# An attention stage ordered by a planner: its delays and occupancies replaced, and 14 transposes of the identity put first

## The chip, the cores and the metric

The kernel runs on one core of a Trainium2 chip. Its time is the device time in microseconds (us) of one execution. Five engines work in parallel, each through its own queue in a fixed order: TensorE (PE, with its weight loads shown as PEld), VectorE (DVE), ScalarE (ACT), GpSimd (POOL), and SyncE (SP), which issues the DMAs. An instruction that has to wait for another engine holds up everything behind it in its queue.

## The reference

Three layers follow each other: attention over pooled queries, a gated layer, and a mixture of eight experts with a routing that is normalised over rows and columns.

```python
q_pool = q.reshape(B, H, S // 2, 2, D).mean(axis=3)      # 2 x 8 heads, 576 pooled rows, 64 columns
scores = (1 / np.sqrt(D)) * np.matmul(q_pool, k.transpose(0, 1, 3, 2))   # 576 x 1152
attn = np.exp(scores - np.max(scores, axis=-1, keepdims=True))
attn = attn / (np.sum(attn, axis=-1, keepdims=True) + 1e-09)
x = np.matmul(attn, v)                                   # to 1152 tokens of 512
gate = 1.0 / (1.0 + np.exp(-(x @ w_gate)))
x = (gate * (x @ w_val)) @ w_out                         # 512 -> 1536 -> 512
...
out += P[:, e:e + 1] * (np.maximum(x @ w1[e], 0.0) @ w2[e])   # e = 0 to 7; P from 8 normalisations
```

## The kernel before

The attention stage takes the heads two by two: eight pairs, numbered 0 to 7. Each matmul operand is kept as a high and a low part, so that a product is two or three matmuls. A pair has nine units of 128 score rows. Unit 0 holds the 64 remainder rows of both heads, units 1 to 4 the other rows of the pair's first head, units 5 to 8 those of its second.

The way of a unit is the same for all. PE multiplies its rows with K in three pieces (step `s`, lines 327 to 334); pieces 0 and 1 go to the PSUM buffer psA, piece 2 to psB. There is one psA and one psB. DVE takes the maximum over psA (`ma`, line 342), ACT the exp of it (`ea`, line 348), and with that psA is free. DVE takes the maximum over psB (`mb`, line 354) and the smaller of the two (`m`, line 360), ACT the exp of psB (`eb`, line 363) and of the difference (`e`, line 370), and POOL brings the first part to the common maximum (`b`, line 374). PE then transposes the result in three groups of three (`tpp`, line 382) into the general PSUM buffers psg, of which there are five. ACT takes the high part out (`ph`, line 398), DVE the low part (`pl`, line 402). These pT tiles are the moving operand of the value matmuls (`pv`, line 421), 18 for each half of a head.

When a half is done, POOL adds up the sums of the exps (`r1`, `r2`, line 434), DVE adds a small constant and takes reciprocals (`r`, lines 439 and 440), PE spreads them (`tr`, line 445), ACT copies one part of the values into a tile sw (`o1`, line 457), DVE adds the other part and multiplies by the reciprocals (`o2`, `o3`, lines 461 to 469), and POOL splits the result into the next layer's x (`xh`, `xl`, lines 71 and 477). There are two sw tiles. Beside this run the loads of the next pairs on SyncE (`lk`, `lq`, `lv`), the pooling of Q (`pq`, line 262), the splits of K (`kh`, `kl`, lines 285 and 292) and V (`vh`, `vl`, lines 71 and 312) and their transposes (`tpq`, `tpk`, lines 266 and 296). For pair 0, DVE and ACT do what POOL does for the others.

The order of all queues in this stage is written out by a planner. Each step has an engine, a due time `when`, the time `takes` for which it holds its engine, the time `lasts` until its result is there, the steps it depends on, and the buffers that it takes and frees. The function `arrange` starts, again and again, the step that can start first, within a horizon of four units. A step on another engine may start when the result is there and a delay `wake` of that engine is over:

```python
own = s["takes"] if u["eng"] == s["eng"] else s["lasts"] + wake[u["eng"]]
u["at"] = max(u["at"], t + own)
```

These numbers set an order and nothing else: at run time each instruction waits for its semaphores. SyncE's loads are ordered by the same planner, by the time at which their buffers come free. The layers after the attention stage (lines 700 on) have an order of their own, which the planner doesn't touch; the first of them begins with the splitting of the gate weights (lines 97 to 120).

Of the kernel before, what the change touches and what calls it, by code (L numbers as in the profile page):

```python
# [8 lines left out]
F32 = mybir.dt.float32  # L9
# [4 lines left out]
ALU = mybir.AluOpType  # L14
AX = mybir.AxisListType
PSUM = bass.MemoryType.PSUM
P = 128
# [12 lines left out]
def moe_stack_kernel(ctx: ExitStack, tc: tile.TileContext, q, k, v, wg1, wv1, wo1, wg2, w1, w2, out):  # L30
# [6 lines left out]
    nc = tc.nc  # L37
# [93 lines left out]
    with ExitStack() as pa:  # L131
# [6 lines left out]
        def slots(pool, n, shape, dt, name):  # L138
# [24 lines left out]
            "sw": slots(pw, 2, [P, HALF[1][1]], F32, "sw"),  # L163
# [8 lines left out]
        def step(name, eng, when, takes, lasts, emit, deps=(), takes_buf=(), frees=()):  # L172


            steps[name] = dict(
                name=name, eng=eng, when=when, takes=takes, lasts=lasts, emit=emit, deps=deps, gets=takes_buf,
                frees=frees, seq=len(steps),
            )

        def arrange():  # L180

            wake = dict(PE=53, ACT=34, DVE=34, POOL=97, SP=100)
# [13 lines left out]
            while len(out) < len(steps):  # L196
# [30 lines left out]
                for u in users.get(s["name"], ()):  # L227
                    own = s["takes"] if u["eng"] == s["eng"] else s["lasts"] + wake[u["eng"]]
# [207 lines left out]
        def reciprocals(i, j, n):  # L436

            rs = have["sum", i][:, 3, columns(j, n)]
            nc.vector.tensor_scalar(out=rs, in0=rs, scalar1=eps, scalar2=None, op0=ALU.add)
            nc.vector.reciprocal(out=rs, in_=rs)  # L440
# [38 lines left out]
        def mm(w):  # L479
            return w / 2.4 + 13.4  # L480

        for i in range(B * NP):
# [47 lines left out]
            for j in range(2):  # L530
# [9 lines left out]
                for g in range(3):  # L540
# [22 lines left out]
                    ("rh", i, j), "POOL", t, 637, 672, lambda i=i, j=j: rem_high(i, j),  # L563
# [7 lines left out]
            for u in range(U):  # L571
                tu = t0 + order.index(u)
                js = (0, 1) if u == 0 else ((u - 1) // QT,)
                for g in range(3):
# [18 lines left out]
                    [("ma", i, u)] + [("ea", i, order[0])] * (u != order[0]),  # L593
                    [("p", ("p", i, u))] + ([("sum", ("sum", i))] if u == order[0] else []), [("A", i, u)],
                )
                step(("mb", i, u), "DVE", ts + 0.02, 564, 647, lambda i=i, u=u: max_b(i, u), [("s", i, u, 2), ("ma", i, u)])
                step(("m", i, u), "DVE", ts + 0.03, 130, 212, lambda i=i, u=u: max_ab(i, u), [("ma", i, u), ("mb", i, u)])
                step(
                    ("eb", i, u), "ACT", ts + 0.04, 632, 662, lambda i=i, u=u: exp_b(i, u), [("m", i, u), ("ea", i, u)],
                    [], [("B", i, u)],  # L600
                )
                step(("e", i, u), "ACT", ts + 0.05, 185, 283, lambda i=i, u=u: exp_ab(i, u), [("m", i, u), ("eb", i, u)], (), [("nm", i, u)])
                step(("b", i, u), "POOL", ts + 0.06, 789, 826, lambda i=i, u=u: bring(i, u), [("e", i, u), ("ea", i, u)])
                for g in range(3):
# [5 lines left out]
                    if u == 0:  # L610
                        step(
                            ("rem", i, g), "ACT", tp + 0.001, 370, 490, lambda i=i, g=g: take_rem(i, g),
                            [("tpp", i, u, g)] + [("rem", i, 0)] * (g > 0), [("rem", ("rem", i))] if g == 0 else [], [("tpp", i, u, g)],
# [5 lines left out]
                        [("tpp", i, u, g)] + [("ph", i, u - tt, 0)] * (tt + g > 0),  # L619
# [475 lines left out]
```

## Time and profile before

| what | value |
|---|---|
| median of 3 runs | 1309.1 us (1308.77 to 1312.93) |
| the profiled execution | 1310.1 us |
| its span, first to last instruction | 1308.3 us |
| PE busy | 1277.9 us (98%) |
| DVE, ACT, POOL busy | 871.8, 555.2, 424.2 us |
| chain that ended last, by engine | PE 87%, DVE 9%, ACT 2% |

Busy time of PE is modelled from pipelined matmuls, so that a PE shown as busy may still lose time between them; a weight load (PEld) that is late shows where the queue stood. Waits are put down to the engine whose semaphore came last by the profile. Where that engine had long been done, it was another one.

### The profile page before, as it was taken

Reading aid. Unit: us, or ns where it says so; the run is one execution under the profiler, and the core shown is the slowest. Engines: PE = TensorE matmul, PEld = TensorE weight load, DVE = VectorE, ACT = ScalarE, POOL = GpSimd, SP = SyncE. Lnnn points to the kernel's source line nnn. Section 1 sums busy time; section 2 is a strip of 40 time slices with the busy share of each in tenths; the row PEclk is TensorE's granted clock in tenths of the full one; section 3 lists DMA queues with packets and bytes.
Section 4 is the critical chain, followed back from the end, with each engine's and each line's share of the span. In section 5 each row is a group of like instructions: output and inputs, shape, how many; then the busy total and the mean of one; then the engine's idle time right before and its main releaser. Section 6 shows DMA issues by size and latency. Waiting matters only on the chain.

```text
span 1308.3 us, 20214 instructions
## 1 busy us (share of the span) xinstructions
PE 1277.9 (98%) x7770; PEld 1173.2 (90%) x7770; DVE 871.8 (67%) x1687; ACT 555.2 (42%) x1223; POOL 424.2 (32%) x495
## 2 busy tenths in 40 slices
PE   7899999998999999999999999999999999999998
PEld 5899898988999999889889989989988988998997
DVE  6998999997666664859557546646645745754643
ACT  7898898984333332523213213223312412421310
POOL 5788787665343433411102012012012102201000
PEclk9999999999999999999999999999999999999999
DMA  5111111112222332111012101111111210210001
GB/s 146 47 55 47 47 49 36 35 33 81 81 86 77 97 97 81 55 59 61 22 49 66 49 26 56 49 33 49 49 46 36 63 34 33 65 44 22 17 1 73
DMA packets 60863, 70.25 MB, mean 54 GB/s; under 512 B 3296, under 2 KB 47328, under 8 KB 60768
## 3 DMA queue, kind: packets, MB, share of 16 engines
q1 hardware_dynamic: 60768, 68.97, 17.1%
q8 instruction: 61, 1.00, 0.3%
q14 instruction: 34, 0.28, 0.1%
HBM read 66.60 MB, written 2.36 MB: 53 GB/s over the span
## 4 chain that ended last, share of the span: by engine, by line
PE 87%; DVE 9%; ACT 2%; issue 1%; DMA 1%; POOL 0%; DVEq 0%; ACTq 0%; POOLq 0%; SPq 0%
PE py L1048 10%; PE py L1049 10%; PE py L1050 10%; PE psb L714 8%; PE psb L712 8%; PE psb L713 7%; PE psg L421 4%; PE psg L382 4%; PE psa L712 2%; PE psa L714 2%; PE psc L712 2%; PE psa L713 2%; PE psc L714 2%; PE psc L713 2%; DVE pT L402 2%; PE pso L712 2%
## 5 line engine op out<-in xcount | busy, mean ns | idle before, releaser
L930 POOL TENSOR_TENSOR sm_w<-raw_w 128x256 f32<-128x256 f32 x64 | 55.3, 865 | 590.8 <-issue 529.9
L1048 PE MATMUL py<-wsp_w,ht 128*128 128x512 f32 x576 | 227.8, 396 | 0.0
L1049 PE MATMUL py<-wsp_w,ht 128*128 128x512 f32 x576 | 227.8, 395 | 0.0
L1050 PE MATMUL py<-wsp_w,ht 128*128 128x512 f32 x576 | 227.8, 395 | 0.0
L1061 DVE SCALAR_TENSOR_TENSOR acc<-py,pr,acc 128x512 f32<-128x512 f32 x126 | 94.4, 749 | 191.8 <-PE py L1050 191.8
L78 ACT ACTIVATE wsp_w<-raw_w 128x1024 fp32r<-128x1024 f32 x32 | 34.0, 1061 | 312.4 <-PE py L1050 274.3
L421 PE MATMUL psg<-pT,vs 128*128 128x256 f32 (+1 forms) x576 | 147.9, 324 | 0.9 <-DVE pT L402 0.8
L1050 PEld LDWEIGHTS py<-wsp_w,ht 128*128 128x128 f32 x576 | 108.3, 188 | 26.2
L1048 PEld LDWEIGHTS py<-wsp_w,ht 128*128 128x128 f32 x576 | 108.3, 188 | 25.4
L1049 PEld LDWEIGHTS py<-wsp_w,ht 128*128 128x128 f32 x576 | 108.3, 188 | 25.4
L382 PE MATMUL psg<-ident,p 128*128 128x128 f32 x648 | 105.7, 273 | 4.5 <-DVE pT L402 3.2
L402 DVE TENSOR_TENSOR pT<-psg,pT 128x384 fp32r<-128x384 f32 x192 | 101.3, 548 | 5.2 <-ACT pT L398 3.8
L984 ACT ACTIVATE ht<-pw 128x576 fp32r<-128x576 f32 x96 | 65.3, 683 | 89.7 <-DVE pw L974 89.6
L714 PE MATMUL psb<-x,w_gv 128*128 128x384 f32 x288 | 97.1, 337 | 3.5 <-POOL w_gv L120 3.5
L421 PEld LDWEIGHTS psg<-pT,vs 128*128 128x128 f32 x576 | 95.2, 189 | 4.5 <-DVE pT L402 1.0
L712 PE MATMUL psb<-x,w_gv 128*128 128x384 f32 x288 | 96.9, 336 | 0.0
L713 PE MATMUL psb<-x,w_gv 128*128 128x384 f32 x288 | 96.8, 336 | 0.0
L974 DVE TENSOR_TENSOR pw<-psb,pw 128x288 f32<-128x288 f32 x192 | 85.6, 451 | 14.5 <-PE psb L714 13.5
L398 ACT ACTIVATE pT<-psg 128x384 fp32r<-128x384 f32 x192 | 90.4, 491 | 7.7 <-PE psg L382 4.4
L382 PEld LDWEIGHTS psg<-ident,p 128*128 128x128 f32 x648 | 79.4, 140 | 10.2 <-POOL sum L434 2.6
L985 DVE SCALAR_TENSOR_TENSOR ht<-pw,ht 128x576 fp32r<-128x576 f32 x96 | 72.8, 759 | 11.2 <-ACT ht L984 10.7
L712 PE MATMUL psb<-xc,w_w 128*128 128x288 f32 x256 | 75.7, 296 | 1.0 <-DVE pw L974 1.0
(205 smaller groups left out, 3381.9 us busy)
## 6 DMA issues: line engine op xcount, KB each, us to landing
raw_w<-in_moe_w_dram SPq DMA_DIRECT2D x64, 512.0 KB, 3.6
raw_gv<-in_moe_w_gate_dram SPq DMA_DIRECT2D x12, 512.0 KB, 3.5
raw_gv<-in_moe_w_val_dram SPq DMA_DIRECT2D x12, 512.0 KB, 3.6
raw_o<-in_moe_w_out_dram SPq DMA_DIRECT2D x12, 512.0 KB, 3.4
kr<-in_k_dram SPq DMA_DIRECT2D x16, 288.0 KB, 3.1
vr<-in_v_dram SPq DMA_DIRECT2D x16, 288.0 KB, 2.8
qr<-in_q_dram SPq DMA_DIRECT2D x16, 256.0 KB, 3.3
out_dram<-acc SPq DMA_DIRECT2D x9, 256.0 KB, 2.0
```

Source lines behind the costliest of these rows:

```text
L382: nc.tensor.transpose(have["tpp", i, u, g][:, n * P:(n + 1) * P], have["p", i, u][:, jj * P:(jj + 1) * P], ident)
L398: nc.scalar.activation(out=p_parts(i, u, g)[0], in_=turned(i, u, g), func=AF.Copy)
L402: nc.vector.tensor_tensor(out=lo, in0=turned(i, u, g), in1=f(hi), op=ALU.subtract)
L421: nc.tensor.matmul(have["pv", i, j, n][:, 0:HALF[n][1]], have["vs", i, j][:, jj].rearrange("p a d -> p (a d)"), have["pT", i, j, n][s][:, ...
L712: nc.tensor.matmul(ps, wh, xh, start=first, stop=False, skip_group_check=more)
L713: nc.tensor.matmul(ps, wh, xl, start=False, stop=False, skip_group_check=more)
L714: return nc.tensor.matmul(ps, wl, xh, start=False, stop=last, skip_group_check=more).ins
L974: ins = nc.vector.tensor_tensor(out=out_[:, cols], in0=ps[key][nb][:, 0:HB], in1=in_[:, cols], op=ALU.add).ins
L1048: nc.tensor.matmul(py, hh, wr[:, 0], start=(x == 0), stop=False)
L1049: nc.tensor.matmul(py, hh, wr[:, 1], start=False, stop=False)
L1050: nc.tensor.matmul(py, hl, wr[:, 0], start=False, stop=(x == 3))
L1061: nc.vector.scalar_tensor_tensor(out=acc[t], in0=py, scalar=pr[:, t, e:e + 1], in1=acc[t], op0=ALU.mult, op1=ALU.add)
```

## The change

The planner gets other numbers. The delays `wake` go from 53, 34, 34 and 97 ns to 145, 80, 40 and 140 for PE, ACT, DVE and POOL. Several `takes` and `lasts` grow: long matmuls, the add of the sums on POOL, the reciprocals, the copy and the division at the end of a half, one copy on POOL. A step that depends on one of its own engine now waits for that one's result and the delay, except on PE and POOL; where only the order matters, the dependence moves to a new list `after`, which counts `takes` alone. The tiles sw become four. The addition of the constant (line 439) is done for two columns and for a third one apart, where there are three. And a step `warm` on PE, with no dependence on data but the identity, transposes the identity 14 times ahead of all else.

```diff
-            "sw": slots(pw, 2, [P, HALF[1][1]], F32, "sw"),
+            "sw": slots(pw, 4, [P, HALF[1][1]], F32, "sw"),
...
-                name=name, eng=eng, when=when, takes=takes, lasts=lasts, emit=emit, deps=deps, gets=takes_buf,
-                frees=frees, seq=len(steps),
+                name=name, eng=eng, when=when, takes=takes, lasts=lasts, emit=emit, deps=(*deps, *after),
+                after=after, gets=takes_buf, frees=frees, seq=len(steps),
...
-            wake = dict(PE=53, ACT=34, DVE=34, POOL=97, SP=100)
+            wake = dict(PE=145, ACT=80, DVE=40, POOL=140, SP=100)
...
-                    own = s["takes"] if u["eng"] == s["eng"] else s["lasts"] + wake[u["eng"]]
+                    own = s["lasts"] + wake[u["eng"]]
+                    if s["name"] in u["after"] or u["eng"] == s["eng"] in ("PE", "POOL"):
+                        own = s["takes"]
...
-            rs = have["sum", i][:, 3, columns(j, n)]
-            nc.vector.tensor_scalar(out=rs, in0=rs, scalar1=eps, scalar2=None, op0=ALU.add)
+            c = columns(j, n)
+            rs = have["sum", i][:, 3, c]
+            for part in (rs[:, 0:2], rs[:, 2:c.stop - c.start])[0:c.stop - c.start - 1]:
+                nc.vector.tensor_scalar(out=part, in0=part, scalar1=eps, scalar2=None, op0=ALU.add)
             nc.vector.reciprocal(out=rs, in_=rs)
...
-            return w / 2.4 + 13.4
+            return w / 2.4 + (17 if w > 400 else 13.4)
...
                 step(
                     ("ea", i, u), "ACT", ts + 0.01, 791, 822, lambda i=i, u=u: exp_a(i, u),
-                    [("ma", i, u)] + [("ea", i, order[0])] * (u != order[0]),
+                    [("ma", i, u)],
                     [("p", ("p", i, u))] + ([("sum", ("sum", i))] if u == order[0] else []), [("A", i, u)],
-                )
...
+                    after=[("ea", i, order[0])] * (u != order[0]),
+                )
...
-                        ("pv", i, j, n, jj, s), "PE", t, mm(w), w / 2.4 + 222,
+                        ("pv", i, j, n, jj, s), "PE", t, mm(w), w / 2.4 + 300,
...
-                        ("r1", i, j, n), "POOL", t - 0.5, 155, 195, lambda i=i, j=j, n=n: total(i, j, n, ALU.mult), need,
+                        ("r1", i, j, n), "POOL", t - 0.5, 275, 195, lambda i=i, j=j, n=n: total(i, j, n, ALU.mult), need,
...
-                        ("r", i, j, n), "DVE", t + 0.001, 230, 330, lambda i=i, j=j, n=n: reciprocals(i, j, n),
+                        ("r", i, j, n), "DVE", t + 0.001, 570 if (j, n) == (0, 1) else 400, 650 if (j, n) == (0, 1) else 480, lambda i=i, j=j, n=n: reciprocals(i, j, n),
...
-                        ("o1", i, j, n), "ACT", t + 0.003, (400, 453)[n], (380, 435)[n],
+                        ("o1", i, j, n), "ACT", t + 0.003, (550, 600)[n], (530, 585)[n],
...
-                        ("o3", i, j, n), "DVE", t + 0.005, 331 + 131 * n, 416 + 131 * n,
+                        ("o3", i, j, n), "DVE", t + 0.005, 460 + 131 * n, 546 + 131 * n,
...
+        def warm():
+            for n in range(14):
+                nc.tensor.transpose(have["warm"][:, 0:P], ident, ident)
+
+        step("warm", "PE", -20, 3200, 3400, warm, (), [("g", "warm")], ["warm"])
```

The copy `rh` on POOL goes from 637 to 752 in the same way, and `mb`, `eb`, `e`, `rem` and `ph` get their order dependences in `after`, as `ea` does.

What this does to the queues is seen in three places. Source lines after the change are two to fifteen higher, and the numbers in buffer names differ.

The first place is SyncE at the start: kr, qr, qm and vr are the loads of K, Q, Q's remainder rows and V for pair 0, and the first of each is the first head's. Before:

```order
1 L249 DMA kr_0_105<-in_k_dram 128x576
2 L239 DMA qr_0_103<-in_q_dram 128x4x128
3 L243 DMA qm_0_104<-in_q_dram 64x128
4 L249 DMA kr_1_106<-in_k_dram 128x576
5 L239 DMA qr_0_103<-in_q_dram 128x4x128
6 L243 DMA qm_0_104<-in_q_dram 64x128
7 L249 DMA vr_0_107<-in_v_dram 128x576
8 L249 DMA vr_1_108<-in_v_dram 128x576
```

And now:

```order
1 L251 DMA kr_0_105<-in_k_dram 128x576
2 L241 DMA qr_0_103<-in_q_dram 128x4x128
3 L245 DMA qm_0_104<-in_q_dram 64x128
4 L251 DMA kr_1_106<-in_k_dram 128x576
5 L251 DMA vr_0_107<-in_v_dram 128x576
6 L251 DMA vr_1_108<-in_v_dram 128x576
7 L241 DMA qr_0_103<-in_q_dram 128x4x128
8 L245 DMA qm_0_104<-in_q_dram 64x128
```

Both loads of V went ahead of the two loads of the second head's Q.

The second place is DVE at the start, from the low part of the first head's Q (ql) to the split of the second head's Q. Before:

```order
4 L277 SCALAR_TENSOR_TENSOR ql_0_113<-psg_2_146,qh_0_110 128x512
5 L262 TENSOR_TENSOR qs_0_109<-qm_0_104 128x128
6 L262 TENSOR_TENSOR qs_0_109<-qr_0_103 128x512
7 L292 TENSOR_TENSOR ks_1_121<-kr_1_106,ks_1_121 128x9x64
8 L342 TENSOR_REDUCE nm_0_131<-psA_0_142 128x1
9 L277 SCALAR_TENSOR_TENSOR qml_0_118<-psg_4_148,qmh_0_116 128x128
10 L354 TENSOR_REDUCE nm_0_131<-psB_0_143 128x1
11 L360 TENSOR_SCALAR nm_0_131<-nm_0_131 128x1
```

And now:

```order
4 L279 SCALAR_TENSOR_TENSOR ql_0_113<-psg_3_149,qh_0_110 128x512
5 L264 TENSOR_TENSOR qs_0_109<-qm_0_104 128x128
6 L294 TENSOR_TENSOR ks_1_121<-kr_1_106,ks_1_121 128x9x64
7 L344 TENSOR_REDUCE nm_0_131<-psA_0_144 128x1
8 L356 TENSOR_REDUCE nm_0_131<-psB_0_145 128x1
9 L279 SCALAR_TENSOR_TENSOR qml_0_118<-psg_0_146,qmh_0_116 128x128
10 L362 TENSOR_SCALAR nm_0_131<-nm_0_131 128x1
11 L264 TENSOR_TENSOR qs_0_109<-qr_0_103 128x512
```

The pooling of the second head's Q (qs from qr, 128x512) went from ahead of the split of the second K (ks_1) to behind the first unit's maxima.

The third place is PE in pair 3, from the second piece of the scores of unit 1 (psA) to its third (psB). The rows between are transposes of pair 2 (from p) and value matmuls (from pT and vs). Before:

```order
480 L333 MATMUL psA_0_142<-kT_0_122,qh_0_110 128x336
481 L334 MATMUL psA_0_142<-kT_0_122,ql_0_113 128x336
482 L421 MATMUL psg_4_148<-pT11_0_101,vs_0_125 128x320
483 L382 MATMUL psg_2_146<-ident_58,p_1_128 128x128 x3
484 L421 MATMUL psg_4_148<-pT10_0_99,vs_0_125 128x320
485 L333 MATMUL psB_0_143<-kT_0_122,qh_0_110 128x480
486 L334 MATMUL psB_0_143<-kT_0_122,ql_0_113 128x480
```

And now:

```order
484 L335 MATMUL psA_0_144<-kT_0_122,qh_0_110 128x336
485 L336 MATMUL psA_0_144<-kT_0_122,ql_0_113 128x336
486 L423 MATMUL psg_3_149<-pT11_0_101,vs_0_125 128x320
487 L423 MATMUL psg_3_149<-pT10_0_99,vs_0_125 128x320
488 L384 MATMUL psg_1_147<-ident_58,p_1_128 128x128 x3
489 L423 MATMUL psg_3_149<-pT11_0_101,vs_0_125 128x320
490 L423 MATMUL psg_3_149<-pT10_0_99,vs_0_125 128x320
491 L384 MATMUL psg_0_146<-ident_58,p_1_128 128x128 x3
492 L423 MATMUL psg_3_149<-pT11_0_101,vs_0_125 128x320
493 L335 MATMUL psB_0_145<-kT_0_122,qh_0_110 128x480
494 L336 MATMUL psB_0_145<-kT_0_122,ql_0_113 128x480
```

Seven rows stand between the two pieces instead of three. From the third piece to the first piece of unit 2 five value matmuls and two groups of transposes follow in both orders. The closing rows of DVE, ACT and POOL, in which the last half's division meets the splitting of the gate weights, have the same order before and now.

## Rows read from the trace of the kernel before

**Rows 1.** Stretches: start:end, length, busy us (instructions) per engine, clock, DMA share.

```profile
12.30:293.00 280.70, 267.67 (x1907) 246.81 (x1908) 255.38 (x559) 250.23 (x668) 214.11 (x292) 1.00 0.17 49
...
306.20:1308.30 1002.10, 995.04 (x5768) 913.16 (x5768) 600.17 (x1098) 293.61 (x534) 197.66 (x182) 1.00 0.17 54
...
5.36:9.40 4.04, 3.92 (x15) 3.15 (x16) 1.46 (x3) 2.58 (x5) 0.44 (x1) 1.00 1.02 337
```

**Rows 2.** Waits of the weight loads, 12.3 to 293 us: total us, times, longest.

```profile
PEld psA L333 <- ACT p L348: 7.0, 12, 1.5
PEld psB L333 <- ACT p L363: 3.0, 7, 1.0
PEld psg L382 <- POOL sum L434: 2.6, 3, 1.0
...
PEld psA L327 <- ACT p L348: 1.7, 1, 1.7
```

**Rows 3.** Timeline of PE, pair 3: start us, us, engine, line, what.

```profile
119.87 0.39 PE L421 MATMUL psg<-pT,vs 128*128 128x320 f32 x1
120.41 0.42 PE L333 MATMUL psA<-kT,qh 128*128 128x336 f32 x1
```

**Rows 4.** Timeline of PE and ACT at the end of the attention stage.

```profile
296.80 2.38 PE L421 MATMUL psg<-pT,vs 128*128 128x256 f32 x18
...
299.16 2.88 PE L421 MATMUL psg<-pT,vs 128*128 128x320 f32 x18
...
299.27 0.38 ACT L457 ACTIVATE sw<-psg 64x256 f32<-64x256 f32 x1 [1.71 <-POOL x L71]
...
306.24 0.69 PE L714 MATMUL psb<-x,w_gv 128*128 128x384 f32 x1 [3.51 <-POOL w_gv L120]
```

**Rows 5.** Timeline of PE at the start.

```profile
5.36 1.51 PE L296 MATMUL psg<-ident,ks 128*128 128x128 f32 x6 [5.36 <-DVE ks L292]
...
9.40 0.32 PE L333 MATMUL psA<-kT,qh 128*128 128x336 f32 x1
...
15.57 0.82 PE L296 MATMUL psg<-ident,ks 128*128 128x128 f32 x6
```

**Rows 6.** Groups by line and shape, 0 to 306.2 us: count, busy us, mean ns, idle before.

```profile
L360 DVE TENSOR_SCALAR nm<-nm 128x1 f32<-128x1 f32 x72 | 15.2, 211 | 1.8
...
L439 DVE TENSOR_SCALAR sum<-sum,eps 128x3 f32<-128x3 f32 x8 | 6.6, 825 | 0.3 <-POOL sum L434 0.2
```

**Rows 7.** SyncE's issues at the start; landing of the Q remainder.

```profile
2.87 0.43 SPq L239 DMA_DIRECT2D qr<-in_q_dram  x1
3.35 0.52 SPq L243 DMA_DIRECT2D qm<-in_q_dram  x1
3.90 1.06 SPq L249 DMA_DIRECT2D vr<-in_v_dram  x2
...
DMA to landing us min/median/max: 3.5/4.1/4.7
```

**Rows 8.** Timeline of POOL and DVE at the start.

```profile
1.01 0.29 POOL masks.py:199 TENSOR_SCALAR_AFFINE_SELECT ident<-ident 128x128 f32<-128x128 f32 x1
...
4.45 0.76 DVE L292 TENSOR_TENSOR ks<-kr,ks 128x576 fp32r<-128x576 f32 x1 [3.46 <-ACT ks L285]
...
9.00 0.77 DVE L262 TENSOR_TENSOR qs<-qm 128x128 f32<-128x128 f32 x1
...
9.71 1.92 POOL L312 TENSOR_TENSOR vs<-vr,vs 128x576 fp32r<-128x576 f32 x1
...
10.29 1.95 DVE L292 TENSOR_TENSOR ks<-kr,ks 128x576 fp32r<-128x576 f32 x1
```

**Rows 9.** Groups by line and shape, 80 to 293 us.

```profile
L374 POOL TENSOR_SCALAR p<-p,sum 128x672 f32<-128x672 f32 x55 | 45.6, 828 | 23.9 <-ACT sum L370 17.0 <-issue 5.0 <-POOL x L477 1.6
L363 ACT ACTIVATE p<-psB,nm 128x480 f32<-128x480 f32 x54 | 35.7, 661 | 5.7 <-DVE nm L360 5.0
L354 DVE TENSOR_REDUCE nm<-psB 128x1 f32<-128x480 f32 x54 | 34.9, 646 | 0.1
```

More of the change, by code (lines that the diff above doesn't have):

```diff
@@ L170, in moe_stack_kernel, with step @@
         steps = {}
-        def step(name, eng, when, takes, lasts, emit, deps=(), takes_buf=(), frees=()):
+        def step(name, eng, when, takes, lasts, emit, deps=(), takes_buf=(), frees=(), after=()):
             steps[name] = dict(
-                name=name, eng=eng, when=when, takes=takes, lasts=lasts, emit=emit, deps=deps, gets=takes_buf,
-                frees=frees, seq=len(steps),
+                name=name, eng=eng, when=when, takes=takes, lasts=lasts, emit=emit, deps=(*deps, *after),
+                after=after, gets=takes_buf, frees=frees, seq=len(steps),
             )
         def arrange():
-            wake = dict(PE=53, ACT=34, DVE=34, POOL=97, SP=100)
+            wake = dict(PE=145, ACT=80, DVE=40, POOL=140, SP=100)
             users, need, ready = {}, {}, {e: [] for e in wake}
@@ L562, in moe_stack_kernel @@
                 step(
-                    ("rh", i, j), "POOL", t, 637, 672, lambda i=i, j=j: rem_high(i, j),
+                    ("rh", i, j), "POOL", t, 752, 672, lambda i=i, j=j: rem_high(i, j),
                     [("rem", i, g) for g in range(3)] + [("ph", i, 3 + 4 * j, 0)],
@@ L612, in moe_stack_kernel @@
                             ("rem", i, g), "ACT", tp + 0.001, 370, 490, lambda i=i, g=g: take_rem(i, g),
-                            [("tpp", i, u, g)] + [("rem", i, 0)] * (g > 0), [("rem", ("rem", i))] if g == 0 else [], [("tpp", i, u, g)],
+                            [("tpp", i, u, g)], [("rem", ("rem", i))] if g == 0 else [], [("tpp", i, u, g)],
+                            after=[("rem", i, 0)] * (g > 0),
                         )
@@ L618, in moe_stack_kernel @@
                         ("ph", i, u, g), "ACT", tp + 0.001, 370, 490, lambda i=i, u=u, g=g: p_high(i, u, g),
-                        [("tpp", i, u, g)] + [("ph", i, u - tt, 0)] * (tt + g > 0),
-                        [(f"pT{n}", ("pT", i, j, n))] if tt == 0 and g == 0 else [],
+                        [("tpp", i, u, g)], [(f"pT{n}", ("pT", i, j, n))] if tt == 0 and g == 0 else [],
+                        after=[("ph", i, u - tt, 0)] * (tt + g > 0),
                     )
```

10 lines of the change are left out of this document (6 added, 4 removed).

## The prediction, on record before the run

> **What bounds the kernel now.** I read the stretches first. From 306.2 us to the end TensorE (PE) is busy for 995.0 of 1002.1 us [rows 1]. The planner that is changed orders nothing there, so only the attention stage, the first 306.2 us, can move. In its even part, 12.3 to 293 us, PE is busy for 267.7 of 280.7 us, VectorE (DVE) for 255.4 and ScalarE (ACT) for 250.2 [rows 1]: three engines near their limit, so a better order can win a few per cent of the stage at most. Next I read who the weight loads wait for, since a late load is where PE's queue stands still: for the score buffers psA and psB, until an exp on ACT has emptied them, 7.0 + 3.0 + 1.7 = 11.7 us [rows 2]. Last, the rows of single waits: for the score group of pair 3, unit 2, the piece before it starts at 119.87 us and takes 0.16 us of the queue [rows 4], but the group starts at 120.41 us, 0.38 us late [rows 3].
>
> **The change, part by part.** *Score groups.* At that place the new order sets between the second piece of scores (unit 1) and the first of unit 2 ten value matmuls and four groups of transposes (the excerpt shows the first seven rows that go ahead of the third piece); before it was seven and three. A value matmul takes 2.88 / 18 = 0.16 us of the queue [rows 4], a group of three transposes half of the 0.82 us of six, 0.41 us [rows 5] (both a little high, since the last one's tail is in). So some 3 x 0.16 + 0.41 = 0.89 us more of other work lie ahead of the group, against a wait of 0.38 us, which is covered. Pairs 2 to 7 all have this order. In other places there is less to win: ahead of unit 1 the work grows by about 0.1 us only. PE does the same work altogether, so a wait that is covered is time saved, unless a DVE or ACT step comes late in turn. Bounds: 0 and -11.7 us. I take half, **-5.9 us**, because one kind of place is covered in full and the other hardly at all.
>
> *Reciprocals.* The add over three columns becomes one over two columns and one over one column, eight times. The three-column add takes 825 ns in the mean, by far more than the smaller shape; a one-column tensor_scalar takes 211 ns, 72 times [rows 6]. If the two-column part takes as long as the old one did, 8 x 0.21 = 1.7 us are added on DVE, at pair boundaries, where DVE has no gap. I take all of it, **+1.7 us**; if two columns took no longer than one, it would be -8 x (0.825 - 2 x 0.21) = -3.2 us.
>
> *Start, loads.* On SyncE's queue the two loads of V go ahead of the second head's two loads of Q. In the trace the four are issued at 2.87 us (Q), 3.35 (its remainder rows) and 3.90 (two of V, 1.06 us) [rows 7]. In the new order V begins at 2.87, the Q loads at 2.87 + 1.06 = 3.93 us, and the remainder's at about 4.4 us. From issue to landing it took up to 4.7 us, with no V ahead of it; so it lands at 4.4 + 4.7 = 9.1 us or a little later, say 9.3 us, where it now lands at about 3.35 + 4.7 = 8.05 us. The pooling of remainder rows on DVE, which starts at 9.00 us [rows 8], waits for it, and behind it on DVE stand the split of the second K and the first max.
>
> *Start, order on DVE.* The second head's pooling, which fills the time from 9.77 to 10.29 us [rows 8], now goes behind the first maximum. The split of the second K, which is 10.29 to 12.24 us long, then follows the remainder pooling at once [rows 8]. It took 1.95 us against 0.76 us for the first K, with POOL's split of V (9.71 us, 1.92 us) beside it [rows 8]. V is issued 1.03 us earlier in the new order, so POOL's piece moves too. The first max then starts between 9.3 + 0.76 = 10.1 us, if the remainder's pooling is short, and 9.3 + 0.77 + 1.95 = 12.0 us, where now the split ends at 12.24 us: -2.1 to -0.2 us, +0.4 us if the landing is 0.6 us later still. I take **-0.7 us**.
>
> *Start, warm transposes.* The identity is ready at 1.30 us [rows 8]. The first six K transposes take 1.51 us, a later six 0.82 us [rows 5]. Fourteen at the first pace take 14 x 1.51 / 6 = 3.5 us: they end by 4.8 us, before 5.36 us, when the first operands come. So they delay nothing. If they leave the clock at its higher level, ten transposes ahead of the first Q save 10 x 0.69 / 6 = 1.1 us there, but the DVE queue then waits for the Q load anyway. Bounds 0 and -1.1 us; I take **-0.4 us**.
>
> In the trace the pace is slow while transposes run, from 5.36 us, and full at 9.40 us, where a score matmul takes 0.32 us [rows 5], although the clock column, where 1.00 is 2.4 GHz, reads 1.00 for the whole stretch [rows 1]. The Trainium skill ("TensorE: Matmul & The Clock Gate", Part 4) says against this change that the full clock does not engage for transposes, which it says do not count as busy in the same way; by that rule the term would be 0 instead of -0.4 us and the forecast 0.4 us higher. The trace cannot settle it, since score matmuls came just before 9.40 us, too.
>
> *Four slots for sw instead of two:* 0 us. The trace names POOL as what the copy at 299.27 us waited 1.71 us for, but the 18 value matmuls that make its input ended at 296.80 + 2.38 = 299.18 us [rows 4]: PE was the one. *The end of the stage:* 0 us. TensorE stands for 3.51 us until the first gate weights are split [rows 4], and the DVE, ACT and POOL rows of that chain have the same order in both.
>
> Sum: -5.9 + 1.7 - 0.7 - 0.4 = -5.3 us. The profiled execution took 1310.1 us, 1.0 us over the median of 1309.1, its span 1308.3; from it the sum gives 1304.8, and for the median **1303.8 us**.
>
> **Rivals.** *DVE takes the wait over.* For it: DVE is busy 91% of the even part, and the scores' maxima, which free nothing until they ran, share its queue with everything else. Against it: the covered waits lie on PE's side, and DVE still has 280.7 - 255.4 = 25 us idle. Then the -5.9 us are gone: 1309.1 + 1.7 - 1.1 = 1309.7 us.
>
> *The softmax comes too late (slower).* Score groups are issued later, their transposes are not. From the third score piece of unit 6 of pair 3 to that unit's first transposes PE has about 7.4 us of work in the old order and 5.7 us in the new one, an estimate from the order's count of instructions at the paces above. The way through is at least 0.32 (the matmul) + 0.65 + 0.21 + 0.66 + 0.83 us = 2.67 us [rows 5, 6, 9], with a short exp of the size of the 0.21 us 2.9 us, and six handovers of 299.27 - 299.18 = 0.09 us [rows 4] make it 3.4 us. Slack falls from 4.0 to 2.3 us, and POOL's split of V (1.92 us at the start) [rows 8] stands ahead of the last step. Where queueing adds over 2.3 us, the transposes wait for POOL, as they do now in three places for 2.6 us, 0.9 us each [rows 2]. Once a pair that is 7 x 0.9 = 6.1 us, and nothing is won: 1309.7 + 6.1 = 1315.8 us.
>
> *The warm transposes do nothing:* the forecast without its last term, 1304.2 us. For it is that score matmuls stand next to the change of pace; against it that far more transposes went ahead of it.
>
> By that rule of the Trainium skill's TensorE page this case is the expected one; no run here shows yet which holds.
>
> **How the numbers follow.** Chances: forecast 0.46, warm transposes in vain 0.15, DVE takes the wait over 0.25, softmax too late 0.14. The likeliest gives 1303.8 us. The range goes down to 1297 us (nine of the 11.7 us covered, the start at -3.2 us; all bounds at once are less likely than 1 in 10) and up to 1313.5 us, most of the way to the slower case. Over 0.3% (3.9 us, about what a measurement of this kernel tells from no change) is below 1305.2 and above 1313.0 us. The first two cases fall below it four times in five: 0.48. The third, and their rest, give 0.35 for no change. The slower case, with a little of the third, gives 0.17.
>
> **What would show it.** Right: the weight loads' waits for psA and psB fall from 11.7 to near 6 us, the attention stage's last matmul before the gate weights comes some 5 us earlier, and the 306 us mark with it; the first K transposes take 0.11 us each; the remainder pooling on DVE waits for a load near 9.3 us; the one-column adds take 0.21 us. Wrong: PE's waits for psA and psB fall, but waits for pT on DVE rise by as much (DVE is the bound), or the transposes' waits for POOL rise above 6 us (the softmax is late); a stretch after 306.2 us that changes by over 1 us would show that something outside the planner moved.

## The result and the profile after

The changed kernel takes **1297.9 us** (median of 4 runs, 1297.52 to 1298.82), the kernel before, run beside it, 1309.6 us (1308.77 to 1312.93). The ratio is 0.9907, with a 95% interval of 0.9889 to 0.9925: 11.7 us faster. The forecast was 5.3 us faster. The sign and the range held; the size was half of what came.

The profiled execution took 1298.8 us, its span is 1296.5 us. The stretches of the changed kernel answer to [rows 1] (start:end, length, busy us per engine, clock, DMA share, GB/s):

```profile
12.30:280.00 267.70, 260.77 (x1908) 245.16 (x1907) 249.45 (x560) 245.71 (x666) 211.75 (x289) 1.00 0.17 51
...
293.70:1296.50 1002.80, 996.19 (x5768) 914.39 (x5768) 600.72 (x1098) 293.87 (x534) 198.12 (x182) 1.00 0.17 54
```

The layers behind the attention stage are what they were (1002.8 us, 1002.1 before). PE's work in the even part is done in 267.7 us instead of 280.7. VectorE (DVE) is busy for 249.5 us there instead of 255.4, with 560 instructions instead of 559. The same work took 5.9 us less of its time; the experiments come back to that.

Next, the waits of PE's weight loads in that part, which answer to [rows 2] (total us, times, longest):

```profile
PEld psA L335 <- ACT p L350: 3.0, 4, 1.5
PEld psA L329 <- ACT p L350: 2.3, 4, 0.6
PEld psg L298 <- DVE pT L404: 2.1, 5, 0.6
PEld psB L335 <- ACT p L365: 1.7, 4, 0.4
PEld psg L384 <- POOL p L376: 1.5, 1, 1.5
```

The three rows of score buffers make 3.0 + 2.3 + 1.7 = 7.0 us. The transposes of the softmax (L384, before L382) wait 1.5 us in the one row left of this size. Of before, three more rows of the same answer as [rows 2] belong here:

```profile
PEld psg L382 <- DVE pT L402: 1.9, 1, 1.9
...
PEld psg L382 <- POOL p L374: 1.3, 1, 1.3
...
PEld psB L327 <- ACT p L363: 0.5, 1, 0.5
```

With the last one the score buffers made 11.7 + 0.5 = 12.2 us before, and the transposes 2.6 + 1.9 + 1.3 = 5.8 us. The forecast had put nothing on the transposes; its slower rival had them grow.

This view leaves out gaps under 0.15 us. An estimate that has them in is taken from the starts in PE's queue, from 12.3 us to the first gate matmul: each step from one start to the next, against the usual step of the same kind behind the same kind. By it the score pieces came 9.4 us less late in all, the transposes of the softmax 4.8 us less, and everything else 1.6 us more. Together that is the 12.6 us by which the stage got shorter.

The start of PE's queue (start us, us, engine, line, what) answers to [rows 5]:

```profile
1.36 3.25 PE L697 MATMUL psg<-ident 128*128 128x128 f32 x14 [1.36 <-POOL ident masks.py:199]
5.27 1.54 PE L298 MATMUL psg<-ident,ks 128*128 128x128 f32 x6 [0.67 <-DVE ks L294]
```

The warm transposes stand where they should, and the first six K transposes still take 1.54 us (1.51 before). On DVE, against [rows 8]:

```profile
10.28 0.41 DVE L264 TENSOR_TENSOR qs<-qm 128x128 f32<-128x128 f32 x1 [1.26 <-DMA wg_sb<-in_moe_w_gate_dram]
10.61 0.74 DVE L294 TENSOR_TENSOR ks<-kr,ks 128x576 fp32r<-128x576 f32 x1
11.28 0.84 DVE L344 TENSOR_REDUCE nm<-psA 128x1 f32<-128x672 f32 x1
```

The pooling of the remainder rows did wait for its load, to 10.28 us rather than 9.3. (The row names a later DMA that ended by then; the load was issued at 4.29 us, and the longest of its line took 5.9 us to land, where 4.7 were reckoned.) The split of the second K took 0.74 us, with POOL's split of V over by then (1.95 us beside it before), so that the first maximum came at 11.28 us instead of 12.16. The stage gained nothing by it: pair 0's first value matmul starts at 32.66 us, where it was 32.54.

The end of the stage answers to [rows 4]:

```profile
289.55 0.42 PE L727 MATMUL psb<-x,w_gv 128*128 128x384 f32 x1
289.81 0.34 PE L728 MATMUL psb<-x,w_gv 128*128 128x384 f32 x1
293.67 0.69 PE L729 MATMUL psb<-x,w_gv 128*128 128x384 f32 x1 [3.52 <-POOL w_gv L120]
294.15 0.52 PE L727 MATMUL psb<-x,w_gv 128*128 128x384 f32 x1
```

The first gate matmul, which closes the stage, starts at 289.55 us, 12.6 us earlier than before:

```profile
302.13 0.42 PE L712 MATMUL psb<-x,w_gv 128*128 128x384 f32 x1
```

Every run below is read by this start too, since it is free of what comes behind it; it comes from one profile of each kernel. The wait of 3.5 us is the same. For 17 matmuls behind it the step from one start to the next is 0.32 us, where later ones have 0.17; in the kernel before it was so for 9.

### The profile page after: what moved, and what is told of

Read it like the earlier page. It is cut to its first block, busy times and chain, and to the rows that moved or that the text cites. A ratio compares the mean times of both kernels' runs of the same rounds, so it can differ in the third digit from the quotient of the medians.

```text
span 1296.5 us, 20214 instructions
## 1 busy us (share of the span) xinstructions
PE 1276.9 (98%) x7784; PEld 1176.8 (91%) x7784; DVE 867.0 (67%) x1695; ACT 551.4 (43%) x1223; POOL 423.8 (33%) x495
## 3 DMA queue, kind: packets, MB, share of 16 engines
HBM read 66.60 MB, written 2.36 MB: 53 GB/s over the span
## 4 chain that ended last, share of the span: by engine, by line
PE 85%; DVE 8%; ACT 4%; issue 1%; DMA 1%; POOL 1%; SPq 0%; ACTq 0%; POOLq 0%; DVEq 0%
PE py L1063 10%; PE py L1064 10%; PE py L1065 10%; PE psb L727 8%; PE psb L729 8%; PE psb L728 8%; PE psg L423 3%; PE psc L727 3%; PE psa L727 3%; PE psc L729 3%; PE psa L729 3%; PE psc L728 2%; PE psa L728 2%; PE psg L384 2%; DVE pT L404 2%; PE pso L728 2%
## 5 line engine op out<-in xcount | busy, mean ns | idle before, releaser
L423 PE MATMUL psg<-pT,vs 128*128 128x256 f32 (+1 forms) x576 | 135.6, 321 | 0.9 <-DVE pT L404 0.7
L384 PE MATMUL psg<-ident,p 128*128 128x128 f32 x648 | 104.5, 273 | 1.0 <-POOL p L376 1.0
L423 PEld LDWEIGHTS psg<-pT,vs 128*128 128x128 f32 x576 | 92.1, 189 | 5.2 <-DVE pT L404 1.4
L384 PEld LDWEIGHTS psg<-ident,p 128*128 128x128 f32 x648 | 78.9, 140 | 4.7 <-POOL p L376 1.7
```

Source lines behind the costliest of these rows:

```text
L384: nc.tensor.transpose(have["tpp", i, u, g][:, n * P:(n + 1) * P], have["p", i, u][:, jj * P:(jj + 1) * P], ident)
L423: nc.tensor.matmul(have["pv", i, j, n][:, 0:HALF[n][1]], have["vs", i, j][:, jj].rearrange("p a d -> p (a d)"), have["pT", i, j, n][s][:, ...
```

## The experiments

**What the small edits carry.** Four kernels, run together. In the first, only the new order of steps is left:

```diff
-            "sw": slots(pw, 4, [P, HALF[1][1]], F32, "sw"),
+            "sw": slots(pw, 2, [P, HALF[1][1]], F32, "sw"),
-            for part in (rs[:, 0:2], rs[:, 2:c.stop - c.start])[0:c.stop - c.start - 1]:
-                nc.vector.tensor_scalar(out=part, in0=part, scalar1=eps, scalar2=None, op0=ALU.add)
+            nc.vector.tensor_scalar(out=rs, in0=rs, scalar1=eps, scalar2=None, op0=ALU.add)
-        step("warm", "PE", -20, 3200, 3400, warm, (), [("g", "warm")], ["warm"])
```

> The changed kernel with its new order of steps, but without the 14 warm transposes, with two slots for sw as before and the reciprocals' add in one piece. Theory A (the order of steps carries all of the gain): within 1 us of the changed kernel's 1297.9 us. Theory B (the small edits carry a part): 1 us or more above it, up to 1304.4 us, which is about the forecast's order and start terms alone (1309.1 - 5.9 - 0.7 = 1302.5 us) with 2 us for a last pair that had gained nothing.

Measured: 1297.5 us (1296.68 to 1297.63); the kernel before, in the same session, 1311.0. Theory A holds: the order of steps carries all of it. The others take one edit back each. Without the last line of that diff:

> The changed kernel without the 14 warm transposes. Theory A (they do nothing; in the changed kernel's profile the first operands' transposes still take 0.213 us each): 1297.9 us, within 0.5 us. Rival (they harm: in the changed kernel the pace of 0.109 us per transpose came at 12.96 us, before the change at about 9.4 us): 1296 to 1297 us, with the fast pace near 9.4 us again. The forecast's own term (they save 0.4, at most 1.1 us): 1298.3 to 1299.0 us.

Measured: 1297.3 us (1296.48 to 1298.61), 0.1 us outside theory A's figure and 0.3 us outside the rival's. The first gate matmul starts at 289.83 us, so the stage gains nothing without them. With the add in one piece:

> The changed kernel with the reciprocals' add over all of its columns in one instruction. The forecast's term (the split costs 1.7 us on DVE): 1296.2 us; the forecast's other bound (it saves 3.2 us): 1301.1 us. From the profiles (the adds over the sums took 13.8 us in 32 instructions before the change and 13.2 us in 40 after it): 1298.5 us, within 0.5 us.

Measured: 1296.8 us (1296.07 to 1297.93). The first gate matmul starts at 289.07 us, against 289.55 of the changed kernel; the two kernels that keep the split and lose something else have 289.83 and 289.49. So the split costs some 0.4 us of the stage, a quarter of the forecast's term and the other way from what I expected of this run: 1298.5 us was a miss. In the changed kernel the two-column adds have a mean of 363 ns, where the kernel before had 24 of them at 299 ns, and eight over three columns at 825 ns [rows 6]:

```profile
L443 DVE TENSOR_SCALAR sum<-sum,eps 128x2 f32<-128x2 f32 x32 | 11.6, 363 | 0.4
...
L443 DVE TENSOR_SCALAR sum<-sum,eps 128x1 f32<-128x1 f32 x8 | 1.6, 200 | 0.0
```

With two slots for sw:

> The changed kernel with two slots for sw, same order of steps. The forecast's term (0 us): 1297.9 us, within 0.5 us. Rival (with the new order the copies out of the value banks come closer together at a pair's end, and would wait for the older halves' slots): each of 8 pair ends loses some 0.2 us, 1299.5 us, and ScalarE's waits at sw name VectorE or POOL.

Measured: 1297.7 us (1297.41 to 1299.03), the first gate matmul at 289.49 us. The forecast's 0 us holds.

This run and the one with the add in one piece also say something on the warm transposes. With two slots for sw:

```profile
1.36 3.25 PE L697 MATMUL psg<-ident 128*128 128x128 f32 x14 [1.36 <-POOL ident masks.py:199]
5.13 0.88 PE L298 MATMUL psg<-ident,ks 128*128 128x128 f32 x6 [0.53 <-DVE ks L294]
5.84 0.60 PE L268 MATMUL psg<-ident,qs 128*128 128x128 f32 x4
```

Six K transposes took 0.88 us here instead of 1.54: the pace of 2.4 GHz, with nothing but transposes ahead of them. The Trainium skill ("TensorE: Matmul & The Clock Gate", Part 4) says that the full clock does not engage for transposes; this trace speaks against it, as far as these transposes run in the mode that the page means, which the trace doesn't tell. But the pace does not come reliably. Of the eleven profiles of this study with the 14 transposes in front, it had come by 5.5 us in five, at 6.9 us in one, and at 13 to 14 us in five; of the seven without them, at 9.3 to 9.4 us in three and at 13.0 to 14.5 us in four. Nor does it last: in four of the six with an early pace PE was back at the slow one for 2 to 3 us between 11 and 17 us. And an early pace is worth nothing to the stage, since its end does not move (289.07 and 289.49 us where it came early, 289.36 to 289.83 where it did not).

**Which part of the planner.** The order has three corrections: the delays `wake`, the occupancies, and the rule for steps of one engine. Each was put alone into the kernel before:

```diff
-            wake = dict(PE=53, ACT=34, DVE=34, POOL=97, SP=100)
+            wake = dict(PE=145, ACT=80, DVE=40, POOL=140, SP=100)
```

> The kernel before with nothing changed but the planner's five handover delays (PE, ACT, DVE, POOL 145, 80, 40, 140 ns), which alone give another order. Theory W (delays that are too short let the planner set score groups and transposes where their data isn't there yet): at least half of the gain, 1305 us or less where the kernel before takes 1311 us. Theory N (it is the occupancies) or R (the rule for one engine's own steps): within 2 us of the kernel before. Rival (half a correction misleads: the planner balances delays against occupancies that are still too short): slower than before, 1313 us or more.

```diff
-                        ("pv", i, j, n, jj, s), "PE", t, mm(w), w / 2.4 + 222,
+                        ("pv", i, j, n, jj, s), "PE", t, mm(w), w / 2.4 + 300,
...
```

> The kernel before with nothing changed but the planner's occupancies and durations (value matmuls, remainder split, sums, reciprocals, the three steps of the output). Theory N: at least half of the gain, 1305 us or less where the kernel before takes 1311 us, since these steps stand at the halves' ends, beside the score groups that waited. Theories W and R: within 2 us of the kernel before.

```diff
-                    own = s["takes"] if u["eng"] == s["eng"] else s["lasts"] + wake[u["eng"]]
+                    own = s["lasts"] + wake[u["eng"]]
+                    if s["name"] in u["after"] or u["eng"] == s["eng"] in ("PE", "POOL"):
+                        own = s["takes"]
```

> The kernel before with nothing changed but the planner's rule for two steps on one engine (data between two steps of ScalarE or VectorE is ready after its duration and the delay, not after the engine's occupancy; a mere order counts the occupancy). Theory R: at least half of the gain, 1305 us or less where the kernel before takes 1311 us. Theories W and N: within 2 us of the kernel before.

And the changed kernel with that rule taken back:

> The changed kernel with the old rule for two steps on one engine, new delays and occupancies kept. If the three corrections add up and the rule carries the third that the other two leave, 1299 to 1303 us; theory R: 1305 us or more; if any consistent set of delays and occupancies will do (W and N together): within 1 us of the changed kernel's 1297.9 us.

Later, the changed kernel with the old delays, and with the old occupancies (these three keep the small edits, which carry nothing):

> The changed kernel with the old handover delays: rule and occupancies only. If the effects add (rule -9, occupancies -5, delays 0): 1297 to 1299 us. If each order's time is a matter of luck beside the rule: anywhere in 1297 to 1304 us, but by theory D not above 1304, since it has few dependent neighbours (23 and 5).

> The changed kernel with the old occupancies: rule and delays only. If the effects add: 1301 to 1304 us. Theory D: it has 32 and 2 neighbours, between the old order's 52 and 32 and the new one's 12 and 3, so 1301 to 1306 us. If the rule were worth nothing without the occupancies: 1309 us or more.

All eight combinations, the kernel before being between 1309.6 and 1311.8 us in the sessions:

| delays | occupancies | old rule: us, first gate matmul at | new rule: us, first gate matmul at |
|---|---|---|---|
| old | old | 1309.6, 302.13 (before) | 1302.7, 294.53 |
| new | old | 1310.7, 302.15 | 1301.2, 291.65 |
| old | new | 1306.8, 298.68 | 1297.2, 288.79 |
| new | new | 1311.1, 302.77 | 1297.9, 289.55 (changed) |

In every row the new rule brings the stage's end forward by 7.6 to 13.2 us. The occupancies bring 3.4 us alone and 2.1 to 5.7 us beside the rule, and nothing beside the new delays without it. The delays bring nothing by themselves; beside the other corrections they move the stage's end by anything from 2.9 us earlier to 4.1 us later. The last two runs came where added effects were expected (1297.2 and 1301.2 us). Theory R holds, alone and in the last kernel of the four: without the rule, corrected delays and occupancies together were worth nothing, where I had thought they might do for 8 to 12 us. Theory W fell. Theory N holds by half: 1306.8 us lies between its 1305 and the other theories' 2 us.

**What the rule does.** It acts only on a step of DVE or ScalarE that reads what another step of the same engine wrote: in this stage, where ScalarE has no such step, above all on the combined max `m` after `mb`, and the division `o3` after the sum `o2`. Whatever else moves, on any engine, follows from these. The old planner let them follow at once. Two stretches of DVE show what that costs on the chip, first of the kernel before, then of the changed one:

```profile
119.74 0.64 DVE L354 TENSOR_REDUCE nm<-psB 128x1 f32<-128x480 f32 x1
120.41 0.21 DVE L360 TENSOR_SCALAR nm<-nm 128x1 f32<-128x1 f32 x1
```

```profile
107.33 0.64 DVE L356 TENSOR_REDUCE nm<-psB 128x1 f32<-128x480 f32 x1
107.89 0.54 DVE L404 TENSOR_TENSOR pT<-psg,pT 128x384 fp32r<-128x384 f32 x1
108.36 0.20 DVE L362 TENSOR_SCALAR nm<-nm 128x1 f32<-128x1 f32 x1
```

Both maxima take 0.64 us. The step that reads the maximum starts 0.67 us after the maximum's start; one that doesn't read it starts 0.56 us after it, while the maximum is still running. Over the whole stage the medians are 681 ns for the readers of the kernel before and 565 ns for the others of the changed one, 116 ns apart; for the division behind the sum, 531 against 408 ns. The kernel before had 50 and 30 such neighbours by the trace, the changed one 12 and 1. At these medians that would be 38 x 0.116 + 29 x 0.123 = 8.0 us of DVE; its busy time in the even part fell by 5.9 us. Part of the difference may be that a step which reads nothing of the one before can be late, too. In the kernel before:

```profile
107.93 0.65 DVE L354 TENSOR_REDUCE nm<-psB 128x1 f32<-128x480 f32 x1
108.61 0.49 DVE L461 TENSOR_TENSOR sw<-psg,sw 64x320 f32<-64x320 f32 x1
```

This output step, on 64 partitions, starts 31 ns behind the end of a maximum that it doesn't read. Behind that maximum 11 of the 60 others in the changed kernel start after its end, 8 of them output steps, and 13 of the 22 in the kernel before, whose median is 677 ns. What holds them was not tried. The Trainium skill ("VectorE: DVE Perf Modes", "The DRAIN you can't avoid") says that the next operation does not start until the pipeline of the one before is empty, but that one which isn't held starts earlier; the row at 107.89 us, 0.08 us ahead of the maximum's end, is of the second kind.

To test it, the changed order was kept and only the neighbours were put together again:

```diff
+            for a, b in (("mb", "m"), ("o2", "o3")):
+                for s in [s for s in line if s["name"][0] == b]:
+                    k = line.index(steps[(a, *s["name"][1:])])
+                    if all(line.index(steps[d]) <= k for d in s["deps"]):
+                        line.remove(s)
+                        line.insert(k + 1, s)
```

> The changed kernel's order of steps, but with each unit's combined max set directly behind the max of its second part, and each half's division directly behind the sum that it reads, where the order's other conditions allow it (72 and 32 such neighbours on VectorE instead of 12 and 3); the other engines' orders stay. Theory D (a VectorE step that reads what the step right before it wrote starts late: 681 ns instead of 565 from the one start to the next for the max, about 531 instead of 408 for the division): 60 x 0.116 + 29 x 0.12 = 10.4 us more work on VectorE; since VectorE has some slack, 4 to 10 us slower than the changed kernel, 1302 to 1308 us. Theory P (it is the order of TensorE's score groups and transposes alone that won): within 1 us of 1297.9 us, or faster, since the exp of the second part gets its maximum earlier.

Measured: 1303.9 us (1302.57 to 1304.73), 6.0 us slower than the changed kernel (of another session), and the first gate matmul at 294.78 us, 5.2 us later. DVE is busy for 254.6 us in the even part (12.3 to 286 us) instead of 249.5. Theory P falls, and the time is within theory D's range. About half of the gain goes, though no other engine's order was touched, and PE's waits come back:

```profile
PEld psA L335 <- ACT p L350: 6.9, 10, 1.5
PEld psg L384 <- DVE pT L404: 2.6, 7, 0.6
PEld psA L329 <- ACT p L350: 2.4, 7, 0.4
PEld psg L298 <- DVE pT L404: 2.3, 5, 0.5
PEld psg L423 <- DVE pT L404: 2.0, 5, 0.9
PEld psg L384 <- POOL p L376: 2.0, 3, 1.1
```

The rows of psA with one of 0.2 us for psB make 9.5 us (7.0 in the changed kernel), the transposes' two rows 4.6 us (1.5).

The other half stays, and the neighbours can't account for it: by the trace this kernel has 70 and 30 of them, more than the kernel before with its 50 and 30, and still its stage ends 7.4 us earlier. This part must lie in where the planner put the other steps; no run takes it apart. Nor does the count of neighbours rank the four kernels with the new rule: 12 and 1, 17 and 2, 23 and 2, 32 and 1 go with first gate matmuls at 289.55, 294.53, 288.79 and 291.65 us.

With the maxima alone (`("mb", "m")` in that loop):

> The changed kernel with only the combined max set directly behind the max of its second part (72 such neighbours instead of 12; the divisions 10 instead of 3). Theory D: 60 x 0.116 + 7 x 0.12 = 7.8 us more on VectorE of the 10.4 us that cost 6.0 us with both put back, so 4.5 us slower than the changed kernel, 1302.4 us. Rival (the division carries it, since the output banks and the value groups wait for it, and an earlier max is only good for the exp): within 1.5 us of 1297.9 us.

Measured: 1300.3 us (1300.00 to 1301.70), the first gate matmul at 292.35 us. Neither figure was right: by the first gate matmul the maxima carry 2.8 of the 5.2 us, and the divisions the rest, although they are fewer. And that rest is not time of DVE, which is busy for 254.8 us here (12.3 to 283.5 us), as long as with both put back. What hangs on the divisions besides was not tried.

The counter-test took neighbours apart in the old order, by moving the next DVE step in between where the planner's times allowed it:

```diff
+                    if x["at"] <= s["at"] + 60:
+                        line.remove(x)
+                        line.insert(k, x)
```

> The kernel before, with the next VectorE step set between a pair of such neighbours, where its data is there by the planner's times: 33 and 14 neighbours instead of 52 and 32, all else as it was. Theory D: (19 + 18) x 0.12 = 4.4 us less work on VectorE, of which 2 to 4.4 us are won: 1307 to 1309 us where the kernel before takes 1311 us. Theory P: within 1 us of the kernel before, or slower, since TensorE's order stays.

Measured: 1315.6 us (1314.24 to 1317.76), ratio 1.0031 (1.0019 to 1.0044): slower, against theory D. The trace says where:

```profile
PEld psB L333 <- ACT p L363: 7.0, 13, 2.8
PEld psA L333 <- ACT p L348: 5.4, 11, 0.9
PEld psg L296 <- DVE sw L466: 3.6, 6, 0.8
```

The waits for psB go from 3.0 to 7.0 us. The likely reason is that a combined max that comes later delays the exp which frees psB, while PE's score groups were still placed for the earlier one. So DVE's steps apart were worth nothing by themselves here. The rule does two things at once, since it tells the planner the real time of the reader: it sets DVE's steps apart, and places the score groups for what that does to the maximum. This run also leaves a rival to theory D: to move DVE's steps against an order that was planned without it may cost time whichever way they go. The 5.1 us more of busy time with the neighbours put back speak for theory D, the divisions' part against it.

**The end of the stage.** The wait of 3.5 us for the first gate weights was left as it was by the change. Two kernels place the weights' conversion earlier:

```diff
-HO = 30
+HO = 60
```

> The changed kernel with the first gate weights' conversion placed earlier among the attention stage's last steps (priority offset 60 instead of 30). The wait of 3.5 us for the first low part of the weights (TensorE, from 289.8 to 293.7 us) gets shorter by 1 to 2 us, and the 0 to 17 matmuls behind it that run at 1.2 GHz (0.32 instead of 0.17 us each) become fewer: 1295 to 1296.5 us. Rival: VectorE's steps of the last pair are pushed back by as much, 1297.9 us or slower.

> The same with an offset of 100: if the wait goes altogether, 3.5 us and up to 2.5 us of slow matmuls less, 1292 to 1294.5 us. Rival: the conversion's 5.8 us of VectorE work now stand ahead of the last pair's own steps, and what the wait loses the last pair gains: 1297 to 1299 us.

Measured: 1298.0 us (1297.21 to 1299.58) and 1299.1 us (1297.53 to 1301.54). With an offset of 60 the wait was no shorter (3.67 us), against what I expected. With an offset of 100:

```profile
292.77 0.42 PE L727 MATMUL psb<-x,w_gv 128*128 128x384 f32 x1
293.03 0.34 PE L728 MATMUL psb<-x,w_gv 128*128 128x384 f32 x1
295.73 0.44 PE L729 MATMUL psb<-x,w_gv 128*128 128x384 f32 x1 [2.36 <-POOL w_gv L120]
```

The wait falls from 3.52 to 2.36 us, and the stage ends 3.2 us later: the rival's case. DVE has no room there: from 270 us on the weight loads of the last value matmuls wait 3.0 us for its pT tiles, where they waited 1.2 us in the changed kernel.

The other loss at that place is the clock. Two stretches behind the wait, of the changed kernel and of the one without warm transposes (columns as above, the clock third from the end):

```profile
293.00:294.00 1.00, 0.33 (x1) 0.33 (x2) 0.97 (x2) 0.00 (x0) 0.61 (x1) 0.50 0.57 126
294.00:295.00 1.00, 1.00 (x4) 1.00 (x4) 0.94 (x3) 0.00 (x0) 0.68 (x1) 0.50 1.04 359
```

```profile
293.00:294.00 1.00, 0.05 (x1) 0.05 (x1) 1.00 (x1) 0.00 (x0) 0.90 (x1) 1.00 0.35 40
294.00:295.00 1.00, 1.00 (x6) 1.00 (x7) 0.94 (x3) 0.00 (x0) 0.40 (x1) 1.00 1.00 341
```

After the same idle time the first fell to 1.2 GHz (0.50) and the second stayed at 2.4. In the profiles 0 to 17 matmuls ran at the lower level behind that wait, each 0.15 us longer: up to 2.6 us between kernels whose stages end at the same time. So the last run fills the wait:

```diff
+        def hold():
+            for n in range(28):
+                nc.tensor.transpose(have["hold"][:, 0:P], ident, ident)
+
+        step("hold", "PE", U * (B * NP) + 20, 3000, 3200, hold, [("tr", B * NP - 1, 1, 1)], [("g", "hold")], ["hold"])
```

> The changed kernel with 28 more transposes of the identity on TensorE behind the last attention step, 28 x 0.109 = 3.05 us, which fill most of the wait for the first gate weights (the two first gate matmuls then run at the end of that wait). Theory (the matmuls at 1.2 GHz behind the wait come from the idle time, and transposes count as work for the clock, as the early pace of two runs with warm transposes says): no or few matmuls of 0.32 us behind the wait, 1 to 2.5 us less, 1295.4 to 1297 us. Rival (transposes do not hold the clock): 9 to 17 slow matmuls again, 1297.5 to 1298.5 us.

Measured: **1295.9 us** (1295.08 to 1296.64), ratio to the kernel before 0.9892 (0.9877 to 0.9906), the fastest median of all.

```profile
289.23 3.22 PE L703 MATMUL psg<-ident 128*128 128x128 f32 x28
292.21 0.42 PE L733 MATMUL psb<-x,w_gv 128*128 128x384 f32 x1
292.46 0.34 PE L734 MATMUL psb<-x,w_gv 128*128 128x384 f32 x1
293.28 0.44 PE L735 MATMUL psb<-x,w_gv 128*128 128x384 f32 x1 [0.47 <-POOL w_gv L120]
293.56 0.34 PE L733 MATMUL psb<-x,w_gv 128*128 128x384 f32 x1
293.73 0.34 PE L734 MATMUL psb<-x,w_gv 128*128 128x384 f32 x1
```

Behind the wait the steps are 0.17 us from the second matmul on. One profile doesn't show that the transposes did it, since two kernels without these transposes (first gate matmul at 289.83 and 288.79 us) had no slow matmul behind the full wait either. Firmer is the mean granted clock of all executions: 1.000 in three of four and 0.998 in the other here, 0.997 in all four of the changed kernel; other kernels reached 1.000 in single executions. The 2.0 us between the two medians come from two sessions and lie near what a median of these runs can tell.

## Why the prediction was wrong in size

- **"I take half, -5.9 us" on the score groups.** The mechanism is right, the size too small: the rows that it was read from fell by 4.7 us, from 11.7 to 7.0, but with the short gaps it was 9.4 us. The row of 0.5 us for psB and the gaps under 0.15 us were not in its bound.
- **The transposes of the softmax had no term.** The prediction had them only in its slower rival, where they grow. They came 4.8 us less late. With the 3.5 us above this is more than the 6.4 us by which the forecast fell short; other steps of PE came a little later.
- **What failed in both: DVE's work was taken as fixed, and the sum had no term for the order of DVE's steps in the even part.** The prediction read DVE's busy time, "DVE still has 280.7 - 255.4 = 25 us idle", and let DVE enter only as a rival that could take the wait over. But 38 + 29 of its steps stopped standing right behind the step whose result they read, and its busy time fell by 5.9 us. Putting such neighbours back cost 6.0 us, 5.2 us of it in the stage; by the starts in PE's queue, 2.1 us of the score pieces' 9.4 and 2.9 us of the transposes' 4.8 came back. That is rather an upper figure for what the change won by it, since 58 maxima were put back where it had taken 38 apart. With them back the score pieces are still 7.3 us less late than before, near the forecast's -5.9 us; what makes up the rest is open. The edit was in the diff: the line `own = s["lasts"] + wake[u["eng"]]`; but of the three order excerpts ahead of the prediction none was of DVE in the even part.
- **Reciprocals, "+1.7 us".** Too dear by four: some 0.4 us. The mean of 825 ns that it was read from holds one add of 2.62 us; the shortest of the eight took 0.21 us.
- **Start, "-0.7 us".** The steps went as told: the remainder pooling waits for its load, and the first maximum comes 0.9 us earlier. The stage had no use for it: 0.
- **Warm transposes, "-0.4 us".** 0, as in the case with a chance of 0.15. In the changed kernel's own profile the faster pace did not come early; where it did, behind transposes alone, the stage ended no earlier.
- **Slots and stage end, 0 us.** Right. The wait at the end is 3.5 us in both.
- **The range, 1297 to 1313.5 us.** It held, in part by luck: its lower end stood for nine covered microseconds, which came, and for 3.2 us at the start, which did not; the transposes of the softmax stood in for them.

## What to carry to other kernels

Busy time of an engine whose instructions overlap is not its load: measure from start to start, and split it by whether the next instruction reads the result. A planner of queues should count a reader's start from the end of the step that it reads, on the same engine too: that correction alone brought the stage's end forward by 7.6 us. To move such steps by hand in an order that was planned without it lost time here, both ways. When an idle stretch of PE can't be filled with work, transposes of the identity may keep its clock up: in the one kernel that tried it the granted clock was higher in all four executions than in any of the changed kernel.

## What was not expected of the hardware

- A DVE step that reads the result of the max over 480 columns right before it starts 35 ns after that one's end; one that doesn't starts 80 ns ahead of it (medians of the changed kernel). But some output steps on 64 partitions started 31 ns after its end without reading it. Behind the sum of the output step the two are 104 ns after its end and about at its end, 123 ns apart from start to start.
- Transposes alone brought PE to the pace of 0.109 us each by 5.5 us in five of eleven profiles with 14 of them in front; in five others it came at 13 to 14 us. The clock column reads 1.00 in both cases.
- The same wait of 3.5 us left PE at 2.4 GHz in two kernels and dropped it to 1.2 GHz for up to 17 matmuls in others.
